# Banded attention heads in 64-key blocks: packed sinks, one step a banded pair, one PSUM tile for the transposes

## The chip, the cores and the metric

The kernel runs on one core of a Trainium2 chip. The metric is device time in microseconds (us) of the whole program; lower is better. The program was timed in six sittings: the kernel before took 223.7 us in the first and 213.5 to 214.9 us in the other five, which ran on four chips (the record of the first doesn't say which chip it was). So each version is compared with runs of the kernel before on the same chip, as a ratio. Runs are labelled fast or slow; only fast runs enter a ratio.

## The reference, cut to what matters

```python
# q, k, v: (4 batches, 8 heads, 768, 64) float32
is_retrieval = [1, 0, 1, 0, 0, 0, 1, 0]; n_sink = 4; window = 64
causal = rel >= 0                                  # rel = query - key
stream_keep = causal & ((key < n_sink) | (rel < window))
mask = causal for a retrieval head, stream_keep for the others
a = softmax(scale * q @ k.T, masked);  x = a @ v   # heads joined: (3072, 512)
for e in range(8):                                 # each token goes to one expert
    out[domain == e] = relu(x[domain == e] @ w1[e]) @ w2[e]
```

Heads 0, 2 and 6 are full causal heads. Heads 1, 3, 4, 5 and 7 are banded: a query sees 64 keys and the 4 sinks. The program does attention first, then stores x, gathers its rows by expert and runs the eight experts. The change touches attention only.

## The kernel before

Heads are worked on in pairs, (0,2), (6,7), (1,3), (4,5), so there are 16 pair stages over four batches: one full pair, one full/banded pair and two banded pairs a batch. In the stage of pair n TensorE computes the scores of n, ScalarE their exponentials; TensorE also transposes q and k of pair n+1 and forms the value products of pair n-1. VectorE copies ("evacuates") the transposes from PSUM, the memory into which TensorE writes, to SBUF, from which it reads them again, scales the value products, and does the routing arithmetic, one item of it a step. GpSimd casts q, k and v.

PSUM has two pools. Pool `ps_s` has three score buffers of two banks each, pool `ps_b` two buffers of one bank:

```python
    ps_s = ctx.enter_context(tc.tile_pool(name="ps_s", bufs=3, space=PSUM))
    ps_b = ctx.enter_context(tc.tile_pool(name="ps_b", bufs=2, space=PSUM))
```

The transposes of q and of k each have a tile of their own from `ps_b`, and their items are handed to different places of the stage:

```python
    def t_items(n):
        items = {}
        for nm, store in (("q", qT), ("k", kT)):
            cell = {}
            def tr(t, nm=nm, store=store, cell=cell):
                if t == 0:
                    cell["ps"] = ps_b.tile([P, 8, P], FP16, tag="b", name=f"tp{nm}_{n}")
                nc.tensor.transpose(out=cell["ps"][:, t, :], ...)
                if t == NSO - 1:
                    d = tpool.tile([P, P, NSO], FP16, tag=f"{nm}T", name=f"{nm}T_{n}")
                    evac = nc.scalar.copy if n == 0 and nm == "q" else nc.vector.tensor_copy
                    evac(out=d[:], in_=cell["ps"][:, 0:NSO].rearrange("d t p -> d p t"))
                    store[n] = d[:].rearrange("d p t -> d (p t)")
            ...
    # the loop over pairs; A, B_ are the value products of the two heads of n - 1
        if n == NPAIR:
            ...
        elif R == 3:                                   # banded pair: three score tiles
            steps = [T["q"] + A, T["k"] + B_]
        else:                                          # five or six score tiles
            h = len(B_) // 2
            steps = [T["q"] + A, T["k"] + B_[:h], B_[h:]]
        for x, step in enumerate(steps):
            if n < NPAIR:
                scores(n, range(2 * x, min(2 * x + 2, R)))
            if n >= 1 and route:
                route.pop(0)()                         # a routing item, on VectorE
            run(step)
```

The softmax here doesn't subtract the row's maximum and nothing guards it: scores larger than these inputs give would overflow.

Of the kernel before, what the change touches and what calls it, by code (L numbers as in the profile page):

```python
# [9 lines left out]
FP16 = mybir.dt.float16  # L10
# [7 lines left out]
P = 128  # L18
# [3 lines left out]
def kernel(  # L22
# [13 lines left out]
    nc = tc.nc  # L36
# [20 lines left out]
    VS = [[7, 1, 4], [3, 5]]  # L57
# [10 lines left out]
    m_band = neg((ii >= jj) & (ii - jj < WIN))  # L68
    m_band0 = neg((ii >= jj) & ((jj < NS) | (ii - jj < WIN)))
# [6 lines left out]
            m_band0,  # L76
            m_band,
            m_band[:, :P],
            m_band,
            m_band,  # L80
            m_band[:, :P],
            m_band[:, P:],
# [7 lines left out]
    C_ID, C_DG, C_M0, C_M1, C_M2, C_ST, C_ON, C_IO = (  # L90
        0, 128, 256, 768, 1280, 1344, 1472, 1474)
# [40 lines left out]
    vs_t = [  # L132
        [cpool.tile([P, len(VS[x]), D + 1], FP16, name=f"vs{i}_{x}") for x in range(2)]
        for i in range(2)
    ]
# [36 lines left out]
    def cast_v(b, pi):  # L172
        if pi == 0:
            ve_t[b] = vepool.tile([P, NSO, H, D + 1], FP16, tag="ve", name=f"ve_{b}")
            nc.gpsimd.memset(ve_t[b][:, :, :, D : D + 1], 1.0)
        hA, hB = PAIRS[pi]
        for hh, h in enumerate((hA, hB)):
            nc.gpsimd.tensor_copy(out=ve_t[b][:, :, h, 0:D], in_=v_t[b, pi][:, hh])  # L178
        for hh, h in enumerate((hA, hB)):
            if not retr[h]:  # L180
                x = 1 if hh and not retr[hA] else 0
                nc.gpsimd.tensor_copy(
                    out=vs_t[b % 2][x][64 * x : 64 * x + NS, VS[x].index(h), :],
                    in_=ve_t[b][0:NS, 0, h, :],
                )

    def load_w(e, which):
# [24 lines left out]
    S_BINS = [  # L212
        [(0, 0, 192), (1, 128, 192), (5, 640, 128)],
        [(2, 256, 192), (3, 384, 192), (4, 512, 128)],
    ]

    def plan(ra, rb):

        tiles = []

        def bin_(col, hh, bn):
            res, c = [], col
            for jt, i0, w in bn:
                res.append((c, hh, jt, i0, w))
                c += w
            return res

        if ra and rb:
            for n in range(5):
                tiles.append((bin_(0, 0, R_BINS[n]) + bin_(512, 1, R_BINS[n]), 0, 1024))  # L230
            tiles.append((bin_(384, 0, R_BINS[5]) + bin_(512, 1, R_BINS[5]), 384, 640))
        elif ra:
            for n in range(2):
                tiles.append((bin_(0, 0, R_BINS[n]) + bin_(512, 1, S_BINS[n]), 0, 1024))
            tiles.append(
                (
                    bin_(0, 0, R_BINS[2])
                    + [(512, 1, 4, 640, 64), (576, 1, "s", 192, 448)],
                    0,
                    1024,  # L240
                )
            )
            tiles.append((bin_(0, 0, R_BINS[3]) + bin_(512, 0, R_BINS[4]), 0, 1024))
            tiles.append(
                (bin_(384, 0, R_BINS[5]) + [(512, 1, "s", 640, 128)], 384, 640)
            )
        else:
            for n in range(2):
                tiles.append((bin_(0, 0, S_BINS[n]) + bin_(512, 1, S_BINS[n]), 0, 1024))
            tiles.append(  # L250
                (
                    [
                        (448, 0, 4, 640, 64),
                        (512, 1, 4, 640, 64),
                        (0, 2, "s", 192, 448),
                        (576, 2, "s", 640, 128),
                    ],
                    0,
                    704,
                )  # L260
            )
        return tiles
# [3 lines left out]
    def col_of(tiles, hh, jt, i):  # L266
        for n, (chunks, c0, c1) in enumerate(tiles):
            for c, h2, j2, i0, w in chunks:
                if (h2 == hh or (h2 == 2 and jt == "s")) and j2 == jt and i0 <= i < i0 + w:
                    return n, c + i - i0  # L270
        raise KeyError((hh, jt, i))
# [5 lines left out]
    def t_items(n):  # L277

        items = {}
        for nm, store in (("q", qT), ("k", kT)):  # L280
            cell = {}

            def tr(t, nm=nm, store=store, cell=cell):
                if t == 0:
                    cell["ps"] = ps_b.tile([P, 8, P], FP16, tag="b", name=f"tp{nm}_{n}")
                nc.tensor.transpose(  # L286
                    out=cell["ps"][:, t, :], in_=qk_t[nm, n][:, t].rearrange("p h d -> p (h d)"), identity=id_sb
                )
                if t == NSO - 1:
                    d = tpool.tile([P, P, NSO], FP16, tag=f"{nm}T", name=f"{nm}T_{n}")  # L290
                    evac = nc.scalar.copy if n == 0 and nm == "q" else nc.vector.tensor_copy
                    evac(out=d[:], in_=cell["ps"][:, 0:NSO].rearrange("d t p -> d p t"))  # L292
                    store[n] = d[:].rearrange("d p t -> d (p t)")

            items[nm] = [lambda t=t, tr=tr: tr(t) for t in range(NSO)]
        return items

    def scores(n, rounds):
        sps = {}

        def putter(sp):
            begun = set()

            def put(c, w, lhsT, rhs, rows=slice(0, P)):
                bank = c // 512
                nc.tensor.matmul(  # L306
                    out=sp[rows, c : c + w],
                    lhsT=lhsT,
                    rhs=rhs,
                    start=bank not in begun,  # L310
                    stop=True,
                    skip_group_check=True,
                )
                begun.add(bank)

            return put

        for r in rounds:
            sp = ps_s.tile([P, 1024], FP32, tag="sp", name=f"sp_{n}_{r}")
            sps[r] = sp, putter(sp)  # L320
            for c, w, col in masks_of(n, r):
                sps[r][1](c, w, id_sb, c16[:, col : col + w])
        for r in rounds:
            chunks, c0, c1 = plans[n % 4][r]
            sp, put = sps[r]
            lists = {0: [], 1: [], 2: []}
            for ch in chunks:
                lists[ch[1]].append(ch)
            order = []
            for a, c in zip(lists[0] + [None] * 8, lists[1] + [None] * 8):  # L330
                order += [x for x in (a, c) if x]
            for c, hh, jt, i0, w in order:
                rows = slice(64 * hh, 64 * hh + 64)
                j0 = 0 if jt == "s" else jt * P
                put(c, w, kT[n][rows, j0 : j0 + P], qT[n][rows, i0 : i0 + w])
            for c, _, jt, i0, w in lists[2]:
                for hh in range(2):
                    rows = slice(64 * hh, 64 * hh + 64)
                    put(c, w, kT[n][rows, 0:64], qT[n][rows, i0 : i0 + w], rows)
# [7 lines left out]
    def masks_of(n, r):  # L347
        ra, rb = (retr[h] for h in PAIRS[n % 4])
        if ra and rb:
            return [(0 if r < 5 else 384, P, C_DG), (512, P, C_DG)]  # L350
        if ra:
            if r < 2:
                return [(0, P, C_DG), (512, 512, (C_M0, C_M1)[r])]
            return [
                [(0, P, C_DG), (512, 64, C_M2)],
                [(0, P, C_DG), (512, P, C_DG)],
                [(384, P, C_DG)],
            ][r - 2]
        if r < 2:
            return [(c, 512, (C_M0, C_M1)[r]) for c in (0, 512)]  # L360
        return [(448, 64, C_M2), (512, 64, C_M2)]

    def av_items(n):
        b, pi = divmod(n, 4)
        tiles = plans[pi]
        items = []
        for hh, h in enumerate(PAIRS[pi]):
            both_s = not any(retr[x] for x in PAIRS[pi])
            mms = []
            if retr[h]:  # L370
                for it in range(NSO):
                    for jt in range(it + 1):
                        mms.append((it, jt, 0, P))
            else:
                for it in range(NSO):
                    mms.append((it, it, 0, P))
                for it in range(2, NSO):
                    mms.append((it, "s", 0, P))
                mms.append((1, "s", 64, P))
                for it in range(1, NSO):  # L380
                    mms.append((it, it - 1, 0, 64))
            cell = {}

            def mm(x, h=h, hh=hh, mms=mms, cell=cell, both_s=both_s):
                it, jt, m0, m1 = mms[x]
                if x == 0:
# [641 lines left out]
```

## Time and profile before

| | before |
|---|---|
| median, lowest, highest of the first three runs | 224.51, 222.9, 225.42 us |
| the profiled run | 227.59 us (slow), span 225.8 us |
| attention: first exponential to the end of the last | 9.2 to 93.0 us |
| first expert's activation | 99.8 us |
| VectorE, ScalarE, TensorE, GpSimd busy | 98.7, 92.1, 187.7, 120.7 us |

The first view is of stretches of the kernel before: one per batch of the attention, and a long stretch of the experts. The columns are the stretch, its length, the busy time of each engine with the number of its instructions, the granted TensorE clock (1.00 is full, and time before the trace's first clock record is counted as full, too), the busy share of the DMA engines (it can pass 1) and GB/s.

```profile
core 0: us, PE busy (x) PEld busy (x) DVE busy (x) ACT busy (x) POOL busy (x), PEclk, DMA share, GB/s
9.17:32.83 23.66, 18.97 (x268) 12.40 (x264) 18.53 (x42) 14.42 (x18) 14.15 (x26) 1.00 1.15 299
32.83:52.73 19.90, 18.47 (x296) 12.41 (x293) 19.59 (x39) 14.31 (x17) 16.36 (x26) 1.00 1.10 299
52.73:72.97 20.24, 19.11 (x321) 12.99 (x317) 16.09 (x38) 14.42 (x17) 11.21 (x23) 1.00 1.12 314
72.97:93.04 20.07, 17.45 (x289) 11.92 (x285) 10.75 (x21) 14.30 (x17) 14.43 (x23) 1.00 0.89 200
128.00:226.00 98.00, 84.39 (x531) 47.36 (x529) 24.59 (x44) 20.10 (x28) 44.32 (x46) 0.94 0.77 185
```

A batch takes about 20 us, and TensorE and VectorE (DVE) are each nearly full in the second one: 18.5 and 19.6 of 19.9 us.

The second view is the list of waits of the kernel before: "engine line waited for: us in total, times, longest us".

```profile
ACT eT L343 <- PE sp L306: 26.0, 20, 3.4
DVE qT L292 <- PE tpq L286: 8.9, 7, 2.1
PE tpk L286 <- DVE qT L292: 1.1, 2, 0.6
PE o_last L745 <- ACT oute_last L753: 6.4, 1, 6.4
```

The exponentials wait 26.0 us for scores. The transposes of k wait almost nothing for the copy of q: 1.1 us. The last line lies at the program's end: there TensorE writes the second half of a PSUM tile whose first half is being read, and waits 6.4 us for the copies of the first half, although the halves do not overlap.

Another view is the timeline of one banded stage of the kernel before (start, duration, engine, line, operation). Rows of GpSimd, weight loads and some others are left out.

```profile
64.69 2.59 ACT L343 ACTIVATE eT<-sp 128x1024 f16<-128x1024 f32 x3 [0.85 <-PE sp L306]
64.74 0.51 PE L286 MATMUL tpq<-c16s,q 128*128 128x128 f16 x6
65.09 0.80 PE L396 MATMUL av<-ve,eT 128*128 128x65 f16 x21
65.29 0.96 DVE L292 COPY qT<-tpq 128x768 f16<-128x768 f16 x1 [1.07 <-PE tpq L286]
...
66.37 0.51 PE L286 MATMUL tpk<-c16s,k 128*128 128x128 f16 x6
...
66.92 0.96 DVE L292 COPY kT<-tpk 128x768 f16<-128x768 f16 x1
...
68.66 0.62 PE L306 MATMUL sp<-qT,kT 64*128 64x192 f16 x12
69.16 1.02 ACT L343 ACTIVATE eT<-sp 128x1024 f16<-128x1024 f32 x1 [1.88 <-PE sp L306]
```

TensorE does value products (65.09) while VectorE copies qT (65.29). The stage lasts 69.16 - 64.69 = 4.5 us.

### The profile page before, as it was taken

Reading aid. Unit: us, or ns where it says so; the run is one execution under the profiler, and the core shown is the slowest. Engines: PE = TensorE matmul, PEld = TensorE weight load, DVE = VectorE, ACT = ScalarE, POOL = GpSimd, SP = SyncE. Lnnn points to the kernel's source line nnn. Section 1 sums busy time; section 2 is a strip of 40 time slices with the busy share of each in tenths; the row PEclk is TensorE's granted clock in tenths of the full one; section 3 lists DMA queues with packets and bytes.
Section 4 is the critical chain, followed back from the end, with each engine's and each line's share of the span. In section 5 each row is a group of like instructions: output and inputs, shape, how many; then the busy total and the mean of one; then the engine's idle time right before and its main releaser. Section 6 shows DMA issues by size and latency. Waiting matters only on the chain. (4 is left out here: it accounts for less than half of the span.)

```text
span 225.8 us, 4791 instructions
## 1 busy us (share of the span) xinstructions
PE 187.7 (83%) x1959; PEld 123.0 (54%) x1959; DVE 98.7 (44%) x200; ACT 92.1 (41%) x120; POOL 120.7 (53%) x170
## 2 busy tenths in 40 slices
PE   0888779989899999289969499999999999998430
PEld 0455455656576675169958495455554564443210
DVE  1448999998977574142110105520244002433210
ACT  2487248855775885115634260025400461000000
POOL 2446768774666884740178743657566403027611
PEclk9999999999999999859997999999999999999955
DMA  6999999999999998399649999996999999704321
GB/s 190 325 298 312 288 299 298 328 291 281 280 343 320 216 249 172 107 170 235 167 90 212 207 256 209 256 219 185 183 185 280 214 220 279 201 17 168 131 93 48
DMA packets 42909, 49.79 MB, mean 220 GB/s; under 512 B 27263, under 2 KB 35712, under 8 KB 42882
## 3 DMA queue, kind: packets, MB, share of 16 engines
q0 software_dynamic: 7936, 26.75, 52.9%
q1 hardware_dynamic: 34802, 22.62, 35.2%
q8 instruction: 17, 0.28, 0.5%
q10 hardware_dynamic: 144, 0.07, 0.2%
q14 instruction: 10, 0.08, 0.1%
HBM read 56.76 MB, written 10.49 MB: 298 GB/s over the span
## 5 line engine op out<-in xcount | busy, mean ns | idle before, releaser
L343 ACT ACTIVATE eT<-sp 128x1024 f16<-128x1024 f32 (+2 forms) x68 | 57.4, 919 | 28.5 <-PE sp L306 26.0
L718 ACT ACTIVATE hT<-h 128x512 f16<-128x512 f32 (+2 forms) x48 | 32.1, 668 | 62.5 <-PE h L711 61.3
L711 PE MATMUL h<-xT,w 128*128 128x256 f16 (+2 forms) x384 | 53.6, 302 | 0.4 <-issue 0.4
L727 POOL DMA_INDIRECT out_dram<-oute,out_i x27 | 27.0, 1001 | 38.7 <-DVE oute L725 33.0
L711 PEld LDWEIGHTS <-w 128*128 128x128 f16 x384 | 40.6, 117 | 11.5 <-issue 0.6
L761 PE MATMUL o<-w,hT 128*128 128x512 f16 x184 | 41.9, 379 | 0.0
L725 DVE COPY oute<-o 128x512 f32<-128x512 f32 x23 | 15.9, 691 | 55.2 <-PE o L761 47.6
L663 POOL DMA_INDIRECT xe<-x_tok,map_i x24 | 24.4, 1019 | 23.7 <-SPq L932 13.1
L396 PE MATMUL av<-ve,eT 128*128 128x65 f16 (+1 forms) x472 | 24.6, 196 | 5.5 <-remote 3.0
L761 PEld LDWEIGHTS <-hT 128*128 128x128 f16 x184 | 17.5, 98 | 19.8 <-issue 0.8
L396 PEld LDWEIGHTS <-eT 128*128 128x128 f16 (+1 forms) x572 | 21.6, 101 | 10.9 <-DVE xb L409 3.9
L306 PE MATMUL sp<-qT,kT 64*128 64x192 f16 (+8 forms) x276 | 23.6, 273 | 2.8 <-DVE kT L292 2.6
L306 PE MATMUL sp<-c16s 128*128 128x128 f16 (+1 forms) x132 | 21.6, 271 | 1.9 <-ACT eT L343 1.7
L158 POOL CAST q<-q 128x768 f16<-128x768 f32 x15 | 12.4, 829 | 15.0 <-DMA q<-in_q_dram 6.4
L178 POOL CAST ve<-v 128x384 f16<-128x384 f32 x32 | 17.0, 558 | 5.5 <-DMA v<-in_v_dram 5.5
L696 DVE COPY xT<-xtp 128x1024 f16<-128x1024 f16 (+1 forms) x16 | 8.8, 552 | 24.0 <-PE xtp L683 24.0
L409 DVE TENSOR_TENSOR xb<-av,rcp 128x384 f16<-128x384 f32 x32 | 17.8, 557 | 1.1
L292 DVE COPY qT<-tpq 128x768 f16<-128x768 f16 x15 | 14.3, 953 | 8.9 <-PE tpq L286 8.9
L158 POOL CAST k<-k 128x768 f16<-128x768 f32 x15 | 13.6, 904 | 7.9 <-PE tpk L286 4.3
L306 PEld LDWEIGHTS <-kT 64*128 64x128 f16 (+1 forms) x276 | 10.8, 96 | 12.4 <-DVE kT L292 4.3
L292 DVE COPY kT<-tpk 128x768 f16<-128x768 f16 x16 | 15.2, 953 | 3.7 <-PE tpk L286 3.7
L753 ACT COPY oute_last<-o_last 128x128 f32<-128x128 f32 x2 | 0.5, 265 | 32.2 <-DVE oute_last L753 32.2
(83 smaller groups left out, 148.4 us busy)
## 6 DMA issues: line engine op xcount, KB each, us to landing
w<-in_moe_w_dram POOLq DMA_DIRECT2D x16, 1024.0 KB
q<-in_q_dram SPq DMA_DIRECT2D x16, 384.0 KB, 5.9
k<-in_k_dram SPq DMA_DIRECT2D x16, 384.0 KB, 6.0
v<-in_v_dram SPq DMA_DIRECT2D x32, 192.0 KB, 5.8
x_tok<-xb SPq DMA_DIRECT2D x4, 768.0 KB, 7.9
out_dram<-oute,out_i POOLq DMA_INDIRECT x27
xe<-x_tok,map_i POOLq DMA_INDIRECT x24
c16s<-c SPq DMA_DIRECT2D x1, 336.5 KB, 5.5
```

Of the source, the lines that this page charges most:

```text
L158: eng.tensor_copy(out=t[:].rearrange("p t h d -> p h t d"), in_=q32_t[nm, n][:])
L178: nc.gpsimd.tensor_copy(out=ve_t[b][:, :, h, 0:D], in_=v_t[b, pi][:, hh])
L292: evac(out=d[:], in_=cell["ps"][:, 0:NSO].rearrange("d t p -> d p t"))
L306: nc.tensor.matmul(out=sp[rows, c : c + w], lhsT=lhsT, rhs=rhs, start=bank not in begun, stop=True, skip_group_check=True,)
L343: nc.scalar.activation(out=eT[n, r // 3][:, r % 3, c0:c1], in_=sp[:, c0:c1], func=AF.Exp, scale=scale)
L396: nc.tensor.matmul(out=ps[m0:m1, it, :], lhsT=eT[n, r // 3][:, r % 3, c : c + w], rhs=rhs, start=(x == 0), stop=(x == len(mms) - 1), skip_ ...
L409: nc.vector.tensor_tensor(out=xb[b][:, :, h * D : (h + 1) * D], in0=ps[:, :, 0:D], in1=rcp[:].unsqueeze(2).to_broadcast([P, NSO, D]), op=A ...
L663: nc.gpsimd.indirect_dma_start(out=xe_of(pr, g), out_offset=None, in_=x_d[0 : 1 + nb * S, :], in_offset=bass.IndirectOffsetOnAxis(ap=map_i ...
L711: nc.tensor.matmul(out=pv[:, a, c0:c1], lhsT=w_t[e, 1][:, c // 2, c % 2, fc * 512 + fr : (fc + 1) * 512 : 4], rhs=xT_t[e][:, c, c0:c1], st ...
L718: nc.scalar.activation(out=hT_t[e][:, 2 * f2 : 2 * f2 + 2, c0:c1], in_=pv[:, :, c0:c1], func=AF.Relu)
L727: inst = nc.gpsimd.indirect_dma_start(out=out, out_offset=bass.IndirectOffsetOnAxis(ap=out_i[:, s : s + 1], axis=0), in_=o[:], in_offset=None,
L761: nc.tensor.matmul(out=ps[:], lhsT=hT_t[e][:, f, g * P : (g + 1) * P], rhs=w_t[e, 2][:, f // 4, f % 4, :], start=(f == 0), stop=(f == 7),)
```

## The change

Intent: do less work for banded heads. A query meets only the two 64-key blocks that its window can touch, stacked in the 128 rows of one column; the four sinks of several query blocks are packed in row groups of 32. A banded pair then needs two score tiles instead of three, in one step instead of two, and 68 exponential instructions become 56. For the upper and lower block to meet v, a copy of v shifted by 64 rows (`vm`) is made on VectorE. To make room on VectorE, q is evacuated on ScalarE in the one-step stages (eight copies). All transposes of a pair go into one two-bank tile of the score pool.

The diff, cut to its core:

```diff
-            ve_t[b] = vepool.tile([P, NSO, H, D + 1], FP16, tag="ve", name=f"ve_{b}")
+            ve_t[b] = vepool.tile([P, NSO, H, D + 2], FP16, tag="ve", name=f"ve_{b}")
+            vm_t[b] = vepool.tile([P, NSO - 1, len(SH), D + 2], FP16, tag="vm", name=f"vm_{b}")
... 20 small sink copies on GpSimd go; six DMAs load the sinks of v; twelve memsets of their six tiles on VectorE
+    def copy_vm(n):
+        for rows, t0 in ((slice(0, 64), 1), (slice(64, P), 0)):
+            nc.vector.tensor_copy(out=vm_t[b][rows, ...], in_=ve_t[b][rows, t0 : t0 + NSO - 1, ...])
... banded plans: two tiles of 1024 columns; pieces of 64x64, 64x128 and 64x32
-    def t_items(n):
-                    cell["ps"] = ps_b.tile([P, 8, P], FP16, tag="b", name=f"tp{nm}_{n}")
+    def transposes(n, q_evac):
+        ps = ps_s.tile([P, 2, 8, P], FP16, tag="sp", name=f"tp_{n}")
+        for x, (nm, store, evac) in enumerate(
+            (("q", qT, q_evac), ("k", kT, nc.vector.tensor_copy))
+        ):
+            for t in range(NSO):
+                nc.tensor.transpose(out=ps[:, x, t, :], ...)
+            d = tpool.tile([P, P, NSO], FP16, tag=f"{nm}T", name=f"{nm}T_{n}")
+            evac(out=d[:], in_=ps[:, x, 0:NSO].rearrange("d t p -> d p t"))
+            store[n] = d[:].rearrange("d p t -> d (p t)")
... the loop
+            q_evac = nc.scalar.copy if R == 1 else nc.vector.tensor_copy
+            tr = [lambda n=n, q_evac=q_evac: transposes(n + 1, q_evac)]
+        steps = {1: [tr + av0 + av1], 2: [tr + av0, av1], 3: [tr, av0, av1]}[R]
+        if n < NPAIR:
+            copy_vm(n)
```

## The prediction

> **What bounds it now.** The change touches only attention: sixteen head-pair stages from 9.2 to 93 us (boundaries from the exponentials in the timeline).
>
> In the windows view VectorE bounds stages 1 to 8: busy 40.9 of the 43.8 us from 15.2 to 59.0, because routing arithmetic (about 18 us) sits on 3.1 us a stage of its own work (two 953 ns evacuations of qT and kT, two reciprocals, two 557 ns scalings). Later, banded pairs take 3.8 to 4.5 us with TensorE busy 3.7 to 4.4 (ScalarE 2.6); full pairs take 5.5 to 6.3 us, near ScalarE's 5.0. DMA is a close second: its share is 1.04 to 1.18, and GpSimd's casts wait 6.4 us for q and 3.0 for k (waits view).
>
> **What changes.**
> - ScalarE: 68 exponentials become 56, -9 us; eight qT evacuations at 0.8 us come, +6.4. Net -2.5, off the path.
> - VectorE loses those eight (-7.6 us) and gains 24 shifted copies of v. The Trainium skill (VectorE: DVE Perf Modes, "The perf-mode tier table") gives 16-bit SBUF copies the 4x mode; no copy here shows it. I estimate 0.25 us for 660 elements, but this trace has 24-element operations of 0.8 to 1.3 us beside running GpSimd casts, so 0.45 each: +10 us. Six memsets at the start (about 4 us, estimated from the 0.27 us memset) fit in VectorE's first wait; 0.3 us may leak.
> - The larger VectorE gain is placing: routing goes one item a step, and steps fall from ten to seven a batch, so it spreads over stages 1 to 12.
> - TensorE: 140 more matmuls. A banded pair has 38 scores and masks instead of 24; mask columns fall from 2176 to 1536, score pieces run at an estimated 35 to 40 ns each, as pairs do now. Net +0.2 us a banded pair, paid back because its stage has one step, with no second 0.4 us wait.
> - GpSimd loses 20 small copies (about 5 us) and gains six small DMAs (about 0.9 us each, three in stage 4).
>
> **On the path.** Taking per stage the larger of VectorE's and TensorE's or ScalarE's time, VectorE's sum over stages 1 to 12 is about 59 us against 63; later banded stages should take 3.8 to 4.2. DMA landings (q of stage 10 lands near 57 us) cap the gain at 4 to 5 us. Attention ends that much earlier; storing x, gathering and the experts follow in a chain, and nearly all carries over.
>
> Predicted: 219.8 us, 80% range 214.5 to 224.8. Faster by over 2%: 0.50; within 2%: 0.44; slower: 0.06.
>
> **What would show it.** 56 exponentials, the last at 87 to 90 us instead of 92.3. Stages 1 to 8 shorten most (43.8 to about 39.5 us), 9 to 12 by under 1 us. VectorE's total stays within 4 us of 98.7. GpSimd's wait for q grows. Shifted copies average 0.25 to 0.6 us. The stretch from 128 us on keeps its length. TensorE busy in banded stages stays above 3.3 us.
>
> **What would make it wrong.** Switching among 64x128, 64x64 and 64x32 tiles: the skill (TensorEngine Tiling, "Key Properties") says a mode switch drains TensorE. If score pieces cost 60 ns, banded stages keep their length and the gain falls to 2 us. Shifted copies held by GpSimd at the head of VectorE's queue would delay kT and do the same. If DMA is less tight than I read, the gain could reach 8 us. Transposes now take a score buffer; full pairs could lengthen.

## The result, and the profile after

| | before | after |
|---|---|---|
| median on the first chip | 223.7 us (221.75 to 225.42, 4 runs) | 253.81 us (251.17 to 254.93, 4 runs) |
| ratio of fast runs | | 1.136, 95% interval 1.122 to 1.150 |
| attention: first exponential, end of the last | 9.2, 93.0 us | 10.7, 123.6 us |
| first expert's activation | 99.8 us | 127.1 us |
| VectorE, ScalarE, TensorE busy | 98.7, 92.1, 187.7 us | 105.3, 90.2, 196.2 us |

A ratio is the mean time of one kernel's fast runs over that of the other's fast runs of the same rounds, so it is not quite the ratio of the medians quoted. The profiled run of the kernel before is a slow one and that of the kernel after a fast one, so single differences of these two traces carry a few us of doubt; the loss is far larger.

The stretches of the kernel after, one per batch and the same 98 us of the experts:

```profile
core 0: us, PE busy (x) PEld busy (x) DVE busy (x) ACT busy (x) POOL busy (x), PEclk, DMA share, GB/s
10.67:40.35 29.68, 23.10 (x303) 14.25 (x299) 13.77 (x31) 14.10 (x16) 16.34 (x27) 1.00 1.20 286
40.35:66.63 26.28, 18.70 (x332) 12.55 (x328) 18.82 (x52) 14.10 (x16) 11.72 (x19) 0.89 0.90 229
66.63:90.69 24.06, 17.88 (x356) 12.33 (x352) 17.91 (x36) 13.99 (x17) 10.59 (x17) 0.97 0.78 211
90.69:123.57 32.88, 22.98 (x312) 15.06 (x309) 17.63 (x38) 13.51 (x15) 18.42 (x23) 0.67 0.65 138
154.00:252.00 98.00, 84.39 (x515) 47.17 (x513) 24.18 (x42) 19.42 (x27) 42.36 (x44) 0.94 0.74 178
```

The experts are untouched: 84.39 us of TensorE work in the stretch in both, and from the first expert's activation to the end 126.0 us before and 125.3 us after. The whole loss is in attention, 4 to 13 us in each batch. In the two middle batches no engine's busy time accounts for it: in the third TensorE is busy 17.9 of 24.1 us where it was 19.1 of 20.2. It is waiting that grew. In the first and the last batch TensorE's busy time grew as well, by 4.1 and 5.5 us; the clock below has a part in that. The DMA share fell in the last three batches, so it is hardly the loads.

The waits of the kernel after:

```profile
ACT eT L346 <- PE sp L335: 57.9, 26, 7.4
PE tp L302 <- ACT qT L308: 16.0, 8, 3.9
PE tp L302 <- DVE qT L308: 12.5, 8, 2.7
DVE kT L308 <- PE tp L302: 25.8, 16, 6.0
POOL q L155 <- issue: 15.7, 6, 4.7
```

Two lines are new: TensorE, about to write the transposes of k into `tp`, waits for the copy of q out of the same tile, 16.0 us where ScalarE makes it and 12.5 us where VectorE does. Their sum, 28.5 us, is about the whole loss. Two other lines follow from it: kT waits for k's transposes, the exponentials wait 57.9 us for scores instead of 26.0. For the line of GpSimd the profile names no releaser.

The timeline of a banded stage of the kernel after shows how one wait is made:

```profile
80.31 1.94 ACT L346 ACTIVATE eT<-sp 128x1024 f16<-128x1024 f32 x2 [0.57 <-PE sp L335]
80.47 0.51 PE L302 MATMUL tp<-c16s,q 128*128 128x128 f16 x6
...
82.13 0.81 ACT L308 COPY qT<-tp 128x768 f16<-128x768 f16 x1
82.99 0.50 PE L302 MATMUL tp<-c16s,k 128*128 128x128 f16 x6 [2.01 <-ACT qT L308]
83.32 0.83 PE L385 MATMUL av<-ve,eT 128*128 128x65 f16 x22
83.59 0.96 DVE L308 COPY kT<-tp 128x768 f16<-128x768 f16 x1 [2.33 <-PE tp L302]
...
85.26 0.87 PE L335 MATMUL sp<-qT,kT 64*128 64x128 f16 x34
85.90 1.94 ACT L346 ACTIVATE eT<-sp 128x1024 f16<-128x1024 f32 x2 [2.96 <-PE sp L335]
```

q is transposed by 80.98, but its copy stands in ScalarE's queue behind the two exponentials of this stage and starts at 82.13. TensorE works in order: the transposes of k wait 2.01 us for the copy, and the value products, which could have run, stand behind them. Then kT is copied, then come the scores. The stage takes 85.90 - 80.31 = 5.6 us instead of 4.5.

The last batch is worse, and adds the granted clock, 0.67 there (in the kernel before the records show no lower clock in attention). The Trainium skill ("TensorE: Matmul & The Clock Gate", section "What's actually happening") says that the array's clock is halved after an idle window of about 3.4 us. The trace agrees only in part. TensorE's longest wait, 3.9 us (110.36 to 114.26), does hold a fall of the clock, at 112.24. But the four other falls in attention (at 43.98, 64.46, 95.18 and 102.00) came during or within 1.3 us of idle stretches of 2.0 to 2.7 us. That waits of TensorE make its later work slower fits this; no run tested it alone. The 1.00 of the first batch can't be trusted, as the first record comes at 30.32 us: six transposes in a row took 0.80 to 0.82 us up to the group at 22.55 and 0.51 or less from 30.39 on. In the kernel before they took 0.82 at 11.83 and 0.51 or less from 15.33 on. So with the change TensorE also stayed slow for longer at the start.

### The profile page after: what moved, and what is told of

Same layout as the page of the kernel before. It is cut to its first block, busy times and chain, and to the rows that moved or that the text cites. A ratio compares the mean times of both kernels' runs of the same rounds, so it can differ in the third digit from the quotient of the medians.

```text
span 252.4 us, 5100 instructions
## 1 busy us (share of the span) xinstructions
PE 196.2 (78%) x2099; PEld 128.6 (51%) x2099; DVE 105.3 (42%) x229; ACT 90.2 (36%) x115; POOL 117.4 (46%) x152
## 5 line engine op out<-in xcount | busy, mean ns | idle before, releaser
L346 ACT ACTIVATE eT<-sp 128x1024 f16<-128x1024 f32 (+2 forms) x56 | 50.9, 953 | 59.8 <-PE sp L335 57.9
L335 PE MATMUL sp<-qT,kT 64*64 64x128 f16 (+6 forms) x436 | 30.3, 281 | 1.8 <-issue 1.1
L302 PE MATMUL tp<-c16s,k 128*128 128x128 f16 x96 | 9.4, 245 | 28.4 <-ACT qT L308 16.0
L308 DVE COPY kT<-tp 128x768 f16<-128x768 f16 x16 | 15.3, 957 | 25.8 <-PE tp L302 25.8
L155 POOL CAST q<-q 128x768 f16<-128x768 f32 x15 | 12.8, 855 | 28.4 <-issue 15.7
L302 PEld LDWEIGHTS <-k 128*128 128x128 f16 x96 | 7.9, 110 | 30.5 <-issue 30.5
L385 PE MATMUL av<-ve,eT 128*128 128x65 f16 (+1 forms) x372 | 22.8, 217 | 0.0
L318 PE MATMUL sp<-c16s 128*128 128x128 f16 (+2 forms) x112 | 20.8, 311 | 1.6 <-ACT eT L346 1.4
L335 PEld LDWEIGHTS <-kT 64*64 64x64 f16 (+2 forms) x436 | 12.9, 108 | 15.3 <-issue 9.2
L155 POOL CAST k<-k 128x768 f16<-128x768 f32 x15 | 12.4, 830 | 15.8 <-PE tp L302 10.0
L689 DVE COPY xT<-xtp 128x1024 f16<-128x1024 f16 (+1 forms) x16 | 8.8, 552 | 24.1 <-PE xtp L676 24.1
L176 POOL CAST ve<-v 128x384 f16<-128x384 f32 x32 | 16.0, 526 | 6.0 <-DMA v<-in_v_dram 6.0
## 6 DMA issues: line engine op xcount, KB each, us to landing
c16s<-c SPq DMA_DIRECT2D x1, 224.5 KB, 5.2
```

Of the source, the lines that this page charges most:

```text
L155: eng.tensor_copy(out=t[:].rearrange("p t h d -> p h t d"), in_=q32_t[nm, n][:])
L302: nc.tensor.transpose(out=ps[:, x, t, :], in_=qk_t[nm, n][:, t].rearrange("p h d -> p (h d)"), identity=id_sb,)
L318: nc.tensor.matmul(out=sp[:, c : c + w], lhsT=id_sb, rhs=c16[:, col : col + w], start=c // 512 not in begun, stop=True, skip_group_check=True,
L335: nc.tensor.matmul(out=sp[o : o + m, c : c + w], lhsT=kT[n][rows, k0 : k0 + m], rhs=qT[n][rows, i0 : i0 + w], start=False, stop=True, skip ...
L346: nc.scalar.activation(out=eT[n, r // 3][:, r % 3, c0:c1], in_=sp[:, c0:c1], func=AF.Exp, scale=scale)
L385: nc.tensor.matmul(out=ps[m0 : m0 + m, it, :], lhsT=eT[n, r // 3][rows, r % 3, c : c + m], rhs=rhs[:, 0 : D + 1], start=(cell["n"] == 1), ...
```

## The experiments

Theory A: the copy of q between the two sets of transposes, in one shared tile, is the loss. Rivals: the q copy's move to ScalarE (B), the small score pieces and the layout itself (C), the transposes' use of a score buffer (D), the order of VectorE's queue and its collisions with GpSimd (E).

All versions gave correct results. They ran in five sittings on four chips, so ratios are given, with the 95% interval. Medians are in us, and the median of before is that of the same sitting. Where an expectation of the first sitting gives us without a ratio, they are meant for the first two kernels' sitting, where the kernel before was about 10 us slower; divided by its 223.7 us they can be held against the ratios.

### Both sets of transposes first (`e1_both_first`; before: 213.63 us)

```diff
                     identity=id_sb,
                 )
+        for x, (nm, store, evac) in enumerate(
+            (("q", qT, q_evac), ("k", kT, nc.vector.tensor_copy))
+        ):
             d = tpool.tile([P, P, NSO], FP16, tag=f"{nm}T", name=f"{nm}T_{n}")
             evac(out=d[:], in_=ps[:, x, 0:NSO].rearrange("d t p -> d p t"))
```

> The changed kernel with one thing moved: the twelve transposes of q and k of a pair are all issued before either of their two evacuations, in the same score buffer. Theory A (the q evacuation stands between the q and the k transposes in one shared buffer, so TensorE waits for it, 28.5 us in all): the two waits at the k transposes (16.0 us for ScalarE, 12.5 us for VectorE) vanish, banded stages fall from about 5.5 to about 4 us, total 216 to 228 us. Theory B (small score pieces and array tile switches make TensorE slower): still over 245 us. Theory C (shifted copies of v block VectorE's queue ahead of kT): still over 240 us.

Measured: 224.56 us, ratio 1.049 (1.038 to 1.060). Most of the loss goes with a change of order alone: same tile, same work, same engines. The expectation's theories B and C (over 1.07) are out; its range for A (216 to 228 us, 0.97 to 1.02) was missed too, so something is left. In its list of waits TensorE's wait for qT before the transposes is gone, and these appear:

```profile
DVE kT L311 <- ACT qT L311: 7.8, 5, 2.6
PE sp L338 <- DVE kT L311: 8.3, 8, 1.5
```

The copy of k on VectorE now waits for the copy of q on ScalarE. Both only read the tile, and still they come one after the other.

### All q copies back on VectorE, the order as in after (`e2_q_on_vector`; before: 213.63 us)

```diff
-            q_evac = nc.scalar.copy if R == 1 else nc.vector.tensor_copy
+            q_evac = nc.vector.tensor_copy
```

> The changed kernel with every qT evacuation on VectorE, order unchanged. Theory A: the wait at the k transposes stays but changes its releaser; in banded stages it is set by how soon VectorE reaches the qT copy (behind two shifted copies and a routing item, and 0.95 us itself), so about 1.2 to 2 us instead of 2.0, total 245 to 258 us. If instead it is ScalarE as such that is overloaded, the time falls under 235 us.

Measured: 238.01 us, ratio 1.112 (1.101 to 1.124). The engine is not the cause: the wait stays, now 21.8 us for VectorE's copy ("PE tp L302 <- DVE qT L308", 15 times), and the ratio is only about 2 points lower than that of the kernel after (1.136, and 1.130 from two fast runs, in other sittings), as expected under A. B explains a small part at most.

### The kernel before with nothing but the shared tile (`e3_before_shared`; before: 213.63 us)

The layout, exponentials and score pieces of before are kept. `t_items` gives way to the `transposes` of after, all copies on VectorE:

```diff
-            steps = [T["q"] + A, T["k"] + B_]
+            steps = [tr + A, B_]
...
-            steps = [T["q"] + A, T["k"] + B_[:h], B_[h:]]
+            steps = [tr + A, B_[:h], B_[h:]]
```

> The kernel before with one part of the change alone: q and k transposed in one step into one shared score buffer, q evacuated between the two (VectorE). Theory A: a wait of TensorE at the k transposes of 1 to 2 us a stage appears (16 to 28 us in all), total 236 to 250 us. Theories B and C, which blame other parts: no more than 228 us.

Measured: 230.4 us, ratio 1.080 (1.071 to 1.090). The shared tile alone makes the old kernel 8% slower, without any of the new layout: its trace has the line "PE tp L283 <- DVE qT L289: 15.5, 14, 1.9". The edit also moves k's transposes ahead of the value products and takes a score buffer; the next run keeps both.

### The same, both sets of transposes first (`e4_before_shared_first`; before: 213.63 us)

The edit is the one of the first experiment, in this kernel.

> The kernel before with the shared score buffer as in e3_before_shared, but both sets of transposes before both evacuations. Theory A: no wait at the k transposes, total 220 to 228 us, near the kernel before. If the shared score buffer itself (one score slot less in rotation) costs the time, it stays near e3_before_shared.

Measured: 216.92 us, ratio 1.006 (0.996 to 1.015). Before and after this edit the kernels differ by 16.0 us in the means of their fast runs (four and two; 13.5 us by the medians) and by nothing but the order of "q transposes, q copy, k transposes, k copy" against "q, k transposes, q copy, k copy". That settles A as the main cause. It also speaks against D in this kernel: the shared tile, which takes one of three score buffers, costs at most about 1.5% (the interval's upper end, from two fast runs) once the order is right.

### The kernel after again (`after_again`; before: 214.86 us)

> The changed kernel once more, to have it on the same chip as the runs beside it. All theories: ratio to the kernel before 1.11 to 1.15, TensorE's wait at the k transposes 26 to 31 us.

Measured: 246.19 us (242.2 to 249.59, four runs, two of them slow). The two fast runs, 242.2 and 243.35 us, are 1.130 times the mean of before, 214.8 us. The wait was 25.6 us (13.8 and 11.8), just under what was expected. The loss is not that of one chip or sitting.

### Both transposes first, kT copied before qT (`e5_k_first`; before: 214.86 us)

```diff
-        for x, (nm, store, evac) in enumerate(
-            (("q", qT, q_evac), ("k", kT, nc.vector.tensor_copy))
+        for x, nm, store, evac in (
+            (1, "k", kT, nc.vector.tensor_copy), (0, "q", qT, q_evac)
         ):
```

> e1_both_first with kT evacuated ahead of qT. In e1_both_first the kT copy on VectorE waited for the qT copy on ScalarE (7.8 us over five stages), which stands behind two exponentials. Theory A2 (the rest of the loss is the same shared buffer, which also orders the two evacuations): that wait goes, banded stages fall from 4.2 us to about 3.6, ratio to the kernel before 0.99 to 1.02 against 1.049. Rival (the rest is the added small pieces or the shifted copies): stays at 1.04 or above.

Measured: 218.54 us, ratio 1.018 (1.010 to 1.026). By fast runs on the same chip that is 24.4 of 28.0 us recovered (242.8 - 218.4, of 242.8 - 214.8). VectorE's copy no longer stands behind ScalarE's exponentials. But the banded stages did not fall to 3.6 us: they take 3.4 to 4.8, the program's last stage apart. This is the best of the mended versions with a sound set of fast runs, and it is still slower than before.

Its timeline shows one more thing, a collision (E). The second of these rows is a routing operation on 28 elements a partition; in another version's trace the same operation took 0.17 us:

```profile
79.54 0.51 DVE L624 SCALAR_TENSOR_TENSOR mu<-mp__208,mu 128x28 int32<-128x28 int32 x1
79.98 4.71 DVE L627 TENSOR_SCALAR mb<-mb 128x28 int32<-128x28 int32 x1
81.02 3.63 POOL L824 MEMSET xe<- 128x1024 f16 x4
```

It lasted 4.71 us and ended 0.04 us after GpSimd's four memsets. The Trainium skill ("SBUF — State Buffer", section "Who interferes with whom") says that VectorE in some modes and GpSimd share a port pair, that the second one blocks until the first is finished, and that `tensor_scalar` is among the operations concerned. The trace fits that at its end; the operation's record starts 1.04 us before the memsets, so which came first is not settled. With one routing item a step and fewer steps, the change moved the end of routing, and shifted copies, into the time of these memsets: in the trace of every version of the new layout but two (those with memsets on VectorE and with transposes ahead in the new order), the kernel after included, at least one VectorE operation there lasted 2.0 to 4.7 us, in those of the old layout none.

### Value products spread over a full pair's steps (`e6_full_steps`; before: 214.86 us)

```diff
-        steps = {1: [tr + av0 + av1], 2: [tr + av0, av1], 3: [tr, av0, av1]}[R]
+        h = len(av1) // 2
+        steps = {1: [tr + av0 + av1], 2: [tr + av0, av1], 3: [tr + av0, av1[:h], av1[h:]]}[R]
```

> e5_k_first with the value products of full pairs spread over the three steps as in the kernel before (first part beside the transposes, the rest halved) instead of none in the first step. If the bare first step is part of the loss, full pairs shorten from about 7 to 6.3 us or less, 2 to 3 us in all (1 to 1.5%); if not, equal to e5_k_first within 0.7%.

Measured: 220.5 us, ratio 1.026 (1.018 to 1.034). No gain over the version it starts from (1.018): full pairs took 6.5 to 6.8 us, after 6.5 to 7.6.

### The same, shifted copies at the end of the stage (`e7_copies_last`; before: 214.86 us)

```diff
-        if n < NPAIR:
-            copy_vm(n)
         for x, step in enumerate(steps):
             ...
             run(step)
+        if n < NPAIR:
+            copy_vm(n)
```

> e6_full_steps with the shifted copies of v issued at the end of a stage, so that kT and the scalings no longer stand behind them in VectorE's queue. Theory C (the copies at the head of VectorE's queue cost time): 2 to 5 us faster than e6_full_steps. Otherwise equal within 1%.

Measured: 224.26 us, ratio 1.034 (1.023 to 1.044); the profiled run was slow. No gain. The test was weak: at the end of one stage the copies still stand ahead of the next stage's kT on VectorE.

### Transposes ahead of the scores in one-step stages (`e8_ahead`; before: 214.76 us)

This one starts from the first experiment.

```diff
+        if R == 1 and n + 1 < NPAIR:
+            run(tr)
+            steps = [av0 + av1]
         if n < NPAIR:
             copy_vm(n)
```

> e1_both_first with the transposes of the next pair issued ahead of a banded pair's scores instead of behind them, so that the two evacuations (still one after the other) run under the scores and the value products. Theory A2 (what is left of the loss in banded stages is the chain transposes, kT, qT, next scores): banded stages 3.3 to 3.8 us, ratio 0.985 to 1.015. Rival (small pieces or VectorE's load set the banded stages): no better than e5_k_first's 1.018.

Measured: 221.32 us, ratio 1.033 (1.024 to 1.041), against 1.049 of its starting point in another sitting. The ratio is the one that the rival expects, but for another reason: in its trace (a slow run) banded stages do fall to 2.6 to 3.5 us, but for one of 4.2, while full pairs take 6.5 to 8.3 us, and the total hardly gains.

### The same, two routing items in stages 2, 3 and 6 (`e9_route_early`; before: 214.76 us)

```diff
-            if n >= 1 and route:
-                route.pop(0)()
+            for _ in range(2 if n in (2, 3, 6) else 1):
+                if n >= 1 and route:
+                    route.pop(0)()
```

> e8_ahead with two routing items a step in three of the one-step stages, so routing ends in stage 10 and no longer meets the 3.6 us of memsets on GpSimd in stages 12 and 13[...]. If that collision is on the path: 2 to 4 us faster than e8_ahead (1 to 2%); if not, equal within 0.7%.

Measured: 226.63 us, ratio 1.058 (1.049 to 1.067): worse. That routing now stands in front of copies that TensorE needs is a reading, not tested; and its trace (a slow run) still has a shifted copy of 2.90 us beside the memsets.

### The new layout with before's transposes (`e10_layout_only`; before: 214.76 us)

Two tiles from `ps_b`, q and k apart, all copies on VectorE, value products head by head, two routing items in a one-step stage:

```diff
+            steps = {
+                1: [T["q"] + av0 + T["k"] + av1],
+                2: [T["q"] + av0, T["k"] + av1],
+                3: [T["q"] + av0, T["k"] + av1[:h], av1[h:]],
+            }[R]
```

> The changed layout of the banded heads (columns, sinks, shifted copies, 56 exponentials, 140 more matmuls) with the kernel before's transposes: q and k in a small buffer each, evacuated by VectorE, value products head by head between them, routing at the old pace. Theory A (all of the loss comes from the shared buffer, not from the layout): ratio 0.97 to 1.015. Theory B or C (layout or shifted copies): 1.03 or more.

Measured: 224.44 us, ratio 1.046 (1.035 to 1.056). By the letter of the expectation this speaks for its theories B or C. It was meant to show the layout alone, but its list of waits has "PE tpk L305 <- DVE qT L311: 11.2, 8, 3.3". The pool has two buffers, so k's transposes take the buffer that q's leave, and the q copy stands behind shifted copies and routing. A tile of its own does not free k from q when the pool is that small; in before, where no shifted copies stand in the queue, the same wait is 1.1 us. So this run doesn't settle what the layout alone costs.

### kT and qT ahead of shifted copies and routing (`e11_evac_before`; before: 214.38 us)

This one starts from the k-first version.

```diff
-        if n < NPAIR:
-            copy_vm(n)
         for x, step in enumerate(steps):
             if n < NPAIR:
                 scores(n, (2 * x, 2 * x + 1))
+            if x == 0:
+                run(tr)
+                step = step[len(tr):]
+                if n < NPAIR:
+                    copy_vm(n)
```

> The version with both sets of transposes first and k evacuated first (ratio to before 1.018 [1.010, 1.026] on another chip), with one more change: in each stage the transposes and their two evacuations are emitted before the shifted copies and the routing item, so on VectorE kT no longer stands behind them. If VectorE's queue order is the rest of the loss, the ratio falls to 0.98 to 1.005, the wait of the q copy on ScalarE for the kT copy (11.9 us there) falls below 5 us, and the last exponential ends before 93 us. If the rest is something else (the collision with GpSimd, the loads, the one-step stages themselves), the ratio stays at 1.012 or more.

Measured: 222.47 us, ratio 1.039 (1.033 to 1.044). A miss: the order I held to be better is not. The wait of the q copy for the kT copy stayed at 10.9 us (6.4 of them at the start, where ScalarE has nothing else to do). VectorE's order by itself is not the rest of the loss.

### The same, every q copy on VectorE (`e12_evac_all_vector`; before: 214.38 us)

The edit is that of the second experiment.

> The same order with every q evacuation on VectorE too, as before had it. Theory that moving eight of them to ScalarE was worth something: VectorE gets 7.6 us more, in stages 1 to 8 where it is fullest, and the ratio is 0.01 or more above that of e11_evac_before. Rival, that the change of engine for reads of one PSUM tile only adds a handover: the ratio is the same within 0.007, or lower.

Measured: 228.0 us, ratio 1.063 (1.058 to 1.069), 0.025 above its starting point on the same chip. So moving the seven q copies to ScalarE is worth 2.5% in this order. In the order of the kernel after it seemed to cost about 2 points (1.136 against 1.112), but these are two sittings and the intervals touch, so the other sign is likely and not shown.

### The same as two above, memsets on VectorE (`e13_memset_vector`; before: 214.38 us)

```diff
-                nc.gpsimd.memset(xe_t[u][:, 0:2, :], 0.0)
+                nc.vector.memset(xe_t[u][:, 0:2, :], 0.0)
```

> The same as e11_evac_before with the four memsets of the gather buffers [...] issued on VectorE, where a memset of that many elements took about 0.5 us. If the collision costs the attention's end 3 to 4 us, the ratio is 0.012 to 0.02 lower than that of e11_evac_before. If the delayed operations were off the path, the ratio is within 0.006 of it.

Measured: 223.55 us, ratio 1.046 (1.041 to 1.051), no better than 1.039. The collision was real, but taking it away did not shorten the program in this order; in the better k-first order it was not tried. The traces would have misled here: attention ended at 94.9 us in this one and at 101.0 us in the one it starts from. But the first is the fastest of its six runs (220.74 us), the second the slowest of its seven (227.01 us). They show another thing: attention ended 6.1 us earlier, and the first expert's activation came only 2.4 us earlier (101.6 against 104.1), so not all of an earlier end is carried over.

### Transposes ahead of the scores, in the new order (`e14_ahead_ordered`; before: 214.38 us)

```diff
         for x, step in enumerate(steps):
+            if x == 0:
+                step = step[len(tr):]
+            if x == 0 and R == 1:
+                run(tr)
             if n < NPAIR:
                 scores(n, (2 * x, 2 * x + 1))
             if x == 0:
-                run(tr)
-                step = step[len(tr):]
+                if R > 1:
+                    run(tr)
```

> The same as e11_evac_before with, in one-step banded stages only, the next pair's transposes ahead of this pair's scores, so that TensorE works on the scores while the evacuations run. If the one-step stage can pay once no wait for an evacuation is left, banded stages take 3.0 to 3.6 us and the ratio is 0.96 to 0.985. If what the banded stages gain is lost again to the loads, the routing and the full pairs, as in the run that did this without the new order (1.033), the ratio is within 0.01 of e11_evac_before.

Measured: 223.96 us, ratio 1.046 (1.040 to 1.052). No gain. In its trace two banded stages together take 5.7 to 6.5 us, after 7.9 to 9.4 in the version it starts from, and full/banded stages of the middle batches take 11.2 and 8.5 us instead of 5.4: what one stage gains the next one loses.

### Own tiles where a stage has several steps (`e15_own_tiles`; before: 213.47 us)

The k-first version, with `t_items` of before in full and full/banded stages, value products there head by head:

```diff
+        if R > 1:
+            T = t_items(n + 1)
+            h = len(av1) // 2
+            steps = {
+                2: [T["q"] + av0, T["k"] + av1],
+                3: [T["q"] + av0, T["k"] + av1[:h], av1[h:]],
+            }[R]
```

> The k-first version, with in the stages of more than one step (full pairs and full/banded pairs) the transposes as before had them: q and k in two tiles of their own from the value products' pool, each followed by half of the value products, all copies on VectorE. The one-step stages are left as they were. If the score buffer held by the transposes is the rest of the loss, full pairs fall from about 7.2 to 5.5 to 6.2 us, the waits of score masks for the qT copy go away, and the ratio to before is 0.98 to 1.005. If the rest is elsewhere (start, one-step stages, loads), the ratio stays at 1.015 or more.

Measured: 218.34 us, ratio 1.021 (1.016 to 1.026). Full pairs take 5.7 to 6.9 us, against 6.5 to 7.6 us in the version it starts from (the 7.2 us of my expectation was read in another trace), and the ratio is no lower than there, 1.018. D is not the rest of the loss either. Its stretches, a fast run at full clock in three batches of four:

```profile
10.38:34.27 23.89, 22.17 (x303) 14.22 (x299) 15.19 (x34) 14.31 (x16) 16.16 (x27) 1.00 1.16 284
34.27:54.21 19.94, 16.89 (x331) 11.80 (x328) 18.75 (x51) 14.21 (x17) 12.56 (x20) 1.00 1.16 292
54.21:73.38 19.17, 17.37 (x355) 12.36 (x352) 18.23 (x39) 14.10 (x16) 9.22 (x15) 1.00 1.13 308
73.38:94.03 20.65, 17.02 (x309) 11.76 (x306) 18.82 (x37) 13.41 (x15) 12.18 (x17) 0.92 0.88 203
```

The four batches sum to 83.65 us; those of the trace before (a slow run) sum to 83.87 us, and those of `e4_before_shared_first` (old layout, a fast run) to 81.9 us. So even without the large wait the new layout buys no time in attention, and it starts 1.2 us later (10.38 against 9.17).

### The same, transposes ahead in one-step stages (`e16_own_tiles_ahead`; before: 213.47 us)

The edit is that of the run with transposes ahead of the scores, for the k-first copies.

> e15_own_tiles with, in one-step stages, the next pair's transposes ahead of this pair's scores. If the loop of transposes, two copies and scores in a row sets the one-step stage, banded stages fall from about 3.9 to 3.0 to 3.5 us (eight of them, seven after the first), and the ratio is 0.012 to 0.025 below that of e15_own_tiles. If the loads, routing or GpSimd's casts take the gain back, the ratio is within 0.007 of e15_own_tiles.

Measured: 224.25 us; five of its six runs were slow, the one fast run took 215.45 us. No ratio could be formed.

### The same, the sink tiles' memsets on GpSimd (`e17_start`; before: 213.47 us)

```diff
-        nc.vector.memset(t[:], 0.0)
+        nc.gpsimd.memset(t[:], 0.0)
...
-        nc.vector.memset(vs_t[r, bh][32 * r : 32 * r + NS, :, D : D + 1], 1.0)
+        nc.gpsimd.memset(vs_t[r, bh][32 * r : 32 * r + NS, :, D : D + 1], 1.0)
```

> e16_own_tiles_ahead with the twelve memsets of the sink tiles on GpSimd, which waits for its first load until 6.7 us anyway. The first exponential starts 0.8 to 1.2 us earlier (10.4 to about 9.4 us) and, if that carries through, the ratio is 0.003 to 0.006 lower. If the first loads or the routing set the pace of batch 0, the ratio is the same within 0.003.

Measured: 219.52 us, ratio 1.013 (1.005 to 1.021), but on two fast runs of six. The first exponential did not move from 10.38 us, and the timeline says why. VectorE's first casts, 0.56 us each in before, now run beside GpSimd's memsets:

```profile
4.44 1.18 DVE L155 CAST q<-q 128x768 f16<-128x768 f32 x1 [3.30 <-DMA q<-in_q_dram]
5.57 1.41 DVE L155 CAST k<-k 128x768 f16<-128x768 f32 x1
```

They start earlier (4.44 us, against 5.77 in the version with own tiles) and last longer. That fits the port pair of the skill's page again.

## Why the prediction was wrong

The prediction was 219.8 us (214.5 to 224.8) on a kernel of 224.5 us; the result was 253.8 us. The step that failed is this one: "Net +0.2 us a banded pair, paid back because its stage has one step, with no second 0.4 us wait." The one step brought a longer wait than the 0.4 us it saved: in the stage shown, 2.01 us at the transposes of k, and 16.0 us in all where ScalarE copies q. Another 12.5 us came where VectorE copies it, in the stages of full and full/banded pairs, for which the prediction had no wait at all. I had counted the q copies that went to ScalarE as work ("off the path") and had not asked who waits for them. My one sentence on the shared tile, "Transposes now take a score buffer; full pairs could lengthen", looked at the buffer count and not at the order inside the tile.

Point by point:

- Attention did not end at 87 to 90 us; the last exponential ended at 123.6. There were 56 of them, as said.
- The bound of before (VectorE and TensorE nearly full, about 20 us a batch) was read rightly. It was not what bounded the changed kernel, which waits.
- VectorE: shifted copies were estimated at 0.25 us alone and 0.45 us in company, 10 us in all. The group of 24 copies took 10.0 us, 0.418 us on average. My estimate of 0.25 us came from the skill's tier table; in the trace the 64x660 copies took 0.355 us, and a single 64x330 copy beside GpSimd's memsets took 2.58 us. So the sum was right in part by luck. Memsets: 2.9 us for the six large ones. VectorE's total rose 6.6 us. My terms sum to +6.4, yet I wrote "within 4 us"; the sum was right and the check was not.
- ScalarE: predicted -2.5 us net, measured 90.2 - 92.1 = -1.9. The exponentials lost 6.5 us (57.4 to 50.9) instead of 9, and seven copies came, not eight (5.6 us).
- TensorE: the worry over 64x128, 64x64 and 64x32 tiles was wrong. In the stage shown 34 pieces took 0.87 us together, about 26 ns each; I had estimated 35 to 40 and feared 60.
- The start: I gave the memsets 0.3 us of leak. The first exponential started 1.5 us later (10.67 against 9.17), 1.2 us of which remain in the versions with both transposes first. Most of that is the shared tile again: there one of the first pair's two copies waits for the other, and with q and k in tiles of their own (`e10_layout_only`) the first exponential started at 9.55 us, 0.4 us later than before.
- GpSimd's wait for q grew, as said (15.0 to 28.4 us of idle time before those casts). Loads ended 5.4 us of it (6.4 before) and TensorE's transposes 6.9 us; for 15.7 us the profile names no releaser. So it wasn't the loads, and that it was the stall of TensorE is shown for a part.
- The experts kept their length, as said: from the first activation to the end 126.0 us before and 125.3 after.

What is shown: the order inside the shared tile is the main cause, by undoing it in the changed kernel (1.130, from two fast runs, to 1.018 on one chip) and by bringing it into the old one (1.080, and 1.006 with the order mended). What is open: the last 2%. Of about 4.4 us (2.1% of 213.5) 1.2 us lie in the start. The rest no run took away: neither VectorE's order, nor the memsets, nor the score buffer, nor the place of the transposes accounts for it by itself. The trace of `e15_own_tiles` shows where much of it lies. The second stages of the first and of the last batch, both full/banded pairs, take 9.3 and 8.5 us, and the same pair 5.5 us in the batches between; in `e4_before_shared_first` the four take 6.8, 5.7, 5.7 and 5.7 us. In the first of them TensorE was still slow (six transposes took 0.82 us up to 22.76, 0.51 from 26.83 on); in the other two shifted copies begun at 79.85 took 4.94 us beside GpSimd's memsets, and the q copy stood behind them until 84.83. No run removed either in that order. And the gain that I expected does not show in any version's time: with 12 exponentials fewer and without the wait, the batches sum to what they did. It is there in part, as the eight banded stages sum to 29.2 us against 31.2 in that fast trace of the old layout, and is lost in those two stages.

Also open is whether the chip needs this wait. q's part of the tile is 2,048 bytes a partition, and so is k's. The Trainium skill ("PSUM — Partial Sum Buffer", sections "Specifications (TRN2)" and "PSUM bank collisions raise a hardware error") says that a bank holds 2 KiB and that two engines on different banks run clean. If the two parts lie in two banks, the wait comes from how the program orders accesses to one tile. No run here took the wait away and kept the order.

## What to carry to other kernels

When two results share one tile, finish all writes into it before the first read, and put first the read whose engine is free: an engine that works in order stops at a write that waits for a read, and everything behind stops with it. When work is moved to an idle engine, ask who waits for it and what it stands behind there, not only how long it takes; here the move was worth 2.5% with one order and seemed to cost about 2 points with the other. And look in the old trace for small instances of what the change does everywhere: one 6.4 us wait at its end was one.

## What the Trainium skill lacked or had wrong

- "Perfetto Trace Analysis", section "Matmuls", says that independent groups should rotate through different banks so that copies overlap. It lacks that two parts of one tile did not overlap here: the transposes of k waited 28.5 us for copies of q from the other part of the tile, and a copy on VectorE waited 7.8 us for a copy on ScalarE though both only read.
- "TensorEngine Tiling (Array Packing)", section "Key Properties", says that changing the tiling mode drains TensorE, without a size. Here 34 score pieces of 64x128, 64x64 and 64x32 took 0.87 us together, about 26 ns each, with whatever switching costs included.
- No page has how much the same kernel's time differs from one chip or sitting to another: the same kernel took 223.7 us in one sitting and 213.5 to 214.9 us in five others, on four chips.
